# Two chunks of an attention and MLP kernel change to a seven-product scheme, with second layers in thirds

## The chip, the cores and the metric

The kernel runs on one core of one Trainium2 chip. The metric is the device time of one execution in microseconds, from runs on the chip; lower is better.

## What is computed

All arrays are float32. Four batches of eight heads (576 rows, head size 64) go through causal attention with a decay, and the 2304 x 512 result through two MLPs (512 to 1536 to 512), the second with an RMS norm ahead and a SiLU gate:

```python
scores = q @ k.T / 8 + (cum[:, None] - cum[None, :])    # cum = cumsum(log(clip(f)))
attn = softmax(where(causal, scores, -1e9)) @ v         # then rows (B*S, H*D) = (2304, 512)
x = ((x @ w_a) * (x @ w_b)) @ w_out                     # MLP 1
xn = x / sqrt(mean(x * x) + 1e-6) * rms_g
g = xn @ w_gate                                         # MLP 2
out = ((g * sigmoid(g)) * (xn @ w_val)) @ w_out2
```

The weights come as 64-bit floats. The kernel turns each granule of 128 x 512 into a high and a low 32-bit part on the chip ("decode"). A product of two such splits is made from three matmuls: high by high, high by low, low by high.

## The kernel before, in words

The rows are cut into five chunks of 576 (as 256 + 320), 512, 448, 320 and 448 (`CHUNKS`, line 23). A phase is one MLP (0 or 1) over one chunk; `PHASES` (line 33) gives their order, and this text writes them as (MLP, chunk). Activations lie transposed: features on partitions, rows as columns. A phase walks 36 granules of weights (`steps`, line 429; `plan_mlp`, line 557): 24 of the first layer, a and b in turn for 12 feature blocks f, and 12 of the second layer, three for each of four blocks of output. For every granule and sub-width the inner `block` (lines 586 to 593) issues 12 matmuls into one PSUM bank, four parts of K by three.

`gate` and `product` (lines 610 and 628) read the banks of a and b, multiply them on DVE, and `split` (line 643) writes a high part (ACT) and a low part (DVE or POOL) into the tiles `g`. All twelve f stay in SBUF until the second layer sums over them in PSUM. `out_1` keeps MLP 1's result in `x1` and adds up squares; `normed` (line 708) makes the norm of a chunk at the start of the next phase, with matmuls against ones, a Newton iteration over full tiles of 128 rows, and a new split. `out_2` sends MLP 2's result out.

`weights` (line 495) decodes a granule at its first use (load, two DVE operations, two on ACT, one on POOL) and saves it in DRAM (`wd`); later phases load it from there, 512 KB each, into a ring of five tiles. Fourteen granules of MLP 2 are decoded early, in phase (0, 1) (`EARLY`, line 39).

Attention (`plan_attention`, line 1026; `unit`, `packed`, `values`) is spread over the phases by `ATT` (line 42): the first 256 rows of batch 0 before the MLPs start, the rest of batch 0 and batch 1 in (0, 0), batches 2 and 3 over the next six phases. Each finished block is split into the tiles `x` of the chunk that it belongs to.

The order on every engine is made when the kernel is built: each operation has a cost, an engine (or a choice of two), a due time and its dependencies, and `Plan.order` (line 226) picks the operation that can start first, by due time among equals. Tiles of one tag are given out in turn. The planner treats POOL and those DVE operations that are marked `port` as excluding each other (lines 242 to 301). DMAs are all issued by SP, in that order, too.

Of the kernel before, what the change touches and what calls it, by code (L numbers as in the profile page):

```python
# [22 lines left out]
CHUNKS = [(0, (256, 320)), (576, (512,)), (1088, (448,)), (1536, (320,)), (1856, (448,))]  # L23
WIDTH = [sum(x) for _, x in CHUNKS]
N0, NMAX = CHUNKS[0][1][0], max(max(x) for _, x in CHUNKS)
PIECES = sorted({0, N0, *WIDTH})
# [6 lines left out]
PHASES = [(0, 0), (0, 1), (1, 0), (0, 2), (1, 1), (0, 3), (1, 2), (0, 4), (1, 3), (1, 4)]  # L33

LAG = 18

SLOT, HAD = [0, 1, 2, 0, 1], {3: 0, 4: 1}

EARLY = {0: 1, 1: 14}
# [3 lines left out]
    (0, ((256, 384), (384, 512), (512, 576)), ((0, 0, LAG, 1.0),), 8),  # L43
    (1, ALL, ((0, LAG, 99, 1.0),), 2),
    (2, ALL[:3], ((1, 0, 99, 0.6), (2, 0, 99, 0.5)), 0),
    (2, ALL[3:], ((3, 0, 99, 0.7), (4, 0, 99, 0.4)), 0),
    (3, ALL[:1], ((4, 18, 99, 1.0),), 0),
    (3, ALL[1:], ((5, 0, 99, 0.6), (6, 0, 99, 0.5)), 0),
# [9 lines left out]
AHEAD = [18000, 20000, 14000, 20000, 14000, 20000]  # L58
# [5 lines left out]
NORM_AT, NORM_STEPS = 6, (6, 10)  # L64
W_BUFS, W32_BUFS, A_BUFS, BP_BUFS = 5, 2, 4, 4
S_BANKS, T_BANKS, PV_BANKS, M_BANKS, BM_BANKS = 3, 1, 1, 3, 2
# [49 lines left out]
def size(c, s):  # L116
    return CHUNKS[c][1][s]


def halves_of(c, a, e):  # L120
    return [s for s in range(len(CHUNKS[c][1])) if a < half(c, s).stop and e > half(c, s).start]

# [193 lines left out]
class Kernel:  # L316
# [6 lines left out]
    def build(self):  # L323
        with ExitStack() as ctx:
            pool = lambda name, **kw: ctx.enter_context(self.tc.tile_pool(name=name, bufs=1, **kw))
            self.const, self.rot = pool("const"), pool("rot")
            self.dram, self.psum = pool("dram", space=DRAM), pool("psum", space=PSUM)
            self.plan = Plan()
# [18 lines left out]
    def m_bank(self):  # L347
        return self.bank("m", M_BANKS, pool=lambda: self.mpsum)


    def constants(self):
        nc, c = self.nc, self.const
        self.spun = self.bp.tile([128, 128], F32, name="spun")
        nc.vector.memset(self.spun, 1.0)
        self.gain = c.tile([128, KT], F32, name="gain")
        self.x1 = c.tile([128, KT, S], F32, name="x1")
# [4 lines left out]
        self.mask = self.causal(c, "mask", 128, 512)  # L361
# [46 lines left out]
    def make_x(self, pool, s):  # L408
        for t in range(2):
            for k in range(KT):  # L410
                n = max(w for w, x in zip(WIDTH, SLOT) if x == s)
                self.X[s, t, k] = pool.tile([128, n], F32R, name=f"x{s}{t}{k}")

    def make_g(self, pool, fs):
        for t in range(2):
            for f in fs:
                self.G[t, f] = pool.tile([128, S], F32R, name=f"g{t}{f}")

    def swap(self):

        for x in self.boot[::-1]:
            x.__exit__(None, None, None)
        self.mpsum = self.ctx.enter_context(self.tc.tile_pool(name="mpsum", bufs=1, space=PSUM))
        pool = self.ctx.enter_context(self.tc.tile_pool(name="late", bufs=1))
        self.make_x(pool, 2)
        self.make_g(pool, range(4, FT))


    def steps(self, p):

        both = tuple(range(len(CHUNKS[PHASES[p][1]][1])))
        if p:
            return [(j, both) for j in range(NG)]
        ab = 2 * FT
        return (
            [(j, both[:1]) for j in range(LAG)] + [(j, both) for j in range(LAG, ab)]
            + [(j, both[1:]) for j in range(LAG)] + [(j, both) for j in range(ab, NG)]
        )

    def weave(self):  # L440
        np_ = len(PHASES)
        blocks = [sum(len(subs) for _, subs in self.steps(p)) for p in range(np_)]
        extra = [[0.0] * n for n in blocks]
        for c, rows, parts, sf in ATT:
            for p, a, e, share in parts:
                span = range(a, min(e, blocks[p]))
# [4 lines left out]
        for p in range(np_):  # L451
            self.T.append([t])
            c = PHASES[p][1]
            for x, s in zip(extra[p], (s for _, subs in self.steps(p) for s in subs)):
                t += 12 * mm(size(c, s)) + x
                self.T[-1].append(t)
        self.x_parts, self.ab_blocks, self.decoded = {}, {}, set()
        self.plan_boot()
        self.op(
            DVE, dve2(128),  # L460
            lambda: self.nc.vector.tensor_scalar(
                out=self.ones, in0=self.ident, scalar1=0.0, scalar2=1.0, op0=ALU.mult, op1=ALU.add
            ),
            writes=["ones"], prio=0, start=40000,
        )
# [28 lines left out]

# [784 lines left out]
```

## Time and profile before

| what | us |
|---|---|
| median of 3 runs | 1123.12 |
| lowest and highest run | 1122.2, 1126.85 |
| span of the profiled execution, first to last instruction | 1120.8 |
| PE busy in it | 1109.3 |

The profile is one execution of the program. Its whole time is not listed apart from its span; the median of the runs is 2.3 us above that span, which is what lies around it. PE is TensorE's matmul stream, PEld its weight loads, DVE the vector engine, ACT the scalar engine, POOL GpSimd and SP the engine that issues the DMAs. Matmul records overlap, since each lasts from its issue to its modelled end while the next already runs. The pace of the stream is thus the distance of starts, not the duration.

### The profile page before, as it was taken

Reading aid. Unit: us, or ns where it says so; the run is one execution under the profiler, and the core shown is the slowest. Engines: PE = TensorE matmul, PEld = TensorE weight load, DVE = VectorE, ACT = ScalarE, POOL = GpSimd, SP = SyncE. Lnnn points to the kernel's source line nnn. Section 1 sums busy time; section 2 is a strip of 40 time slices with the busy share of each in tenths; the row PEclk is TensorE's granted clock in tenths of the full one; section 3 lists DMA queues with packets and bytes.
Section 4 is the critical chain, followed back from the end, with each engine's and each line's share of the span. In section 5 each row is a group of like instructions: output and inputs, shape, how many; then the busy total and the mean of one; then the engine's idle time right before and its main releaser. Section 6 shows DMA issues by size and latency. Waiting matters only on the chain.

```text
span 1120.8 us, 19350 instructions
## 1 busy us (share of the span) xinstructions
PE 1109.3 (99%) x7012; PEld 999.3 (89%) x7012; DVE 556.8 (50%) x1481; ACT 466.4 (42%) x1076; POOL 198.7 (18%) x245
## 2 busy tenths in 40 slices
PE   9999999999999999999999999999999999999998
PEld 7677999988889999989988778999889999999997
DVE  7877657747753877234247442544751121360330
ACT  8767557736543565333234332443441121231220
POOL 3323325412231244211011121210200000000000
PEclk9999999999999999999999999999999999999999
DMA  7879886777997488976664568787556767789774
GB/s 224 285 247 303 308 262 213 261 268 278 334 310 273 144 286 278 312 214 196 205 192 164 178 210 258 244 253 224 173 186 197 233 220 215 247 295 311 219 218 153
DMA packets 91220, 268.73 MB, mean 240 GB/s; under 512 B 14444, under 2 KB 27964, under 8 KB 91124
## 3 DMA queue, kind: packets, MB, share of 16 engines
q1 hardware_dynamic: 91124, 267.48, 73.8%
q8 instruction: 56, 0.92, 0.3%
q14 instruction: 40, 0.33, 0.1%
HBM read 224.31 MB, written 43.13 MB: 239 GB/s over the span
## 4 chain that ended last, share of the span: by engine, by line
PE 92%; DVE 4%; DMA 2%; ACT 1%; issue 0%; SPq 0%; POOL 0%; ACTq 0%; POOLq 0%
PE m L591 26%; PE m L593 26%; PE m L592 26%; PE pv L1202 4%; PE t L819 3%; PE s L1119 3%; PE s L1141 2%; PE warm L832 1%; DMA kb<-aux 1%; DMA raw<-wb 1%; DMA raw<-wa 0%; DMA qr<-qT 0%; DVE P L777 0%; DVE x L761 0%; DVE x L655 0%
## 5 line engine op out<-in xcount | busy, mean ns | idle before, releaser
L591 PE MATMUL m<-x,w 128*128 128x320 f32 (+3 forms) x1152 | 399.0, 346 | 1.2 <-DVE a L633 1.0
L593 PE MATMUL m<-x,w 128*128 128x320 f32 (+3 forms) x1152 | 388.3, 337 | 0.0
L592 PE MATMUL m<-x,w 128*128 128x320 f32 (+3 forms) x1152 | 388.0, 337 | 0.0
L591 PEld LDWEIGHTS m<-x,w 128*128 128x128 f32 x1152 | 217.1, 188 | 20.3 <-issue 4.7
L593 PEld LDWEIGHTS m<-x,w 128*128 128x128 f32 x1152 | 216.9, 188 | 13.8
L592 PEld LDWEIGHTS m<-x,w 128*128 128x128 f32 x1152 | 217.3, 189 | 13.1 <-issue 0.5
L591 PE MATMUL m<-g,w 128*128 128x320 f32 (+3 forms) x576 | 197.5, 343 | 0.0
L593 PE MATMUL m<-g,w 128*128 128x320 f32 (+3 forms) x576 | 194.1, 337 | 0.0
L592 PE MATMUL m<-g,w 128*128 128x320 f32 (+3 forms) x576 | 194.0, 337 | 0.0
L633 DVE TENSOR_TENSOR a<-m,a 128x320 f32<-128x320 f32 (+3 forms) x144 | 79.7, 555 | 175.2 <-PE m L593 167.5
L649 ACT ACTIVATE g<-a 128x320 fp32r<-128x320 f32 (+3 forms) x144 | 75.0, 521 | 157.3 <-DVE a L633 157.1
L505 POOL TENSOR_TENSOR w<-w,w 128x512 fp32r<-128x512 f32 x72 | 98.8, 1375 | 219.3 <-ACT w L502 170.0
L615 ACT ACTIVATE a<-m 128x320 f32<-128x320 f32 (+3 forms) x144 | 70.3, 489 | 112.3 <-PE m L593 111.0
L591 PEld LDWEIGHTS m<-g,w 128*128 128x128 f32 x576 | 108.6, 188 | 8.0 <-issue 1.2
L593 PEld LDWEIGHTS m<-g,w 128*128 128x128 f32 x576 | 108.5, 188 | 6.8
L592 PEld LDWEIGHTS m<-g,w 128*128 128x128 f32 x576 | 108.6, 189 | 6.4
L652 DVE TENSOR_TENSOR g<-a,g 128x320 fp32r<-128x320 f32 (+3 forms) x139 | 84.4, 608 | 50.5 <-ACT g L649 49.7
L784 ACT ACTIVATE P<-P,mn 128x512 f32<-128x512 f32 (+4 forms) x128 | 76.1, 595 | 37.2 <-DVE mn L777 36.8
L777 DVE CUSTOM_DVE_ANT_0 P<-s,mask 128x512 f32<-128x512 f32 (+4 forms) x128 | 61.7, 497 | 48.3 <-PE s L1141 24.1
L1183 ACT ACTIVATE pt<-t 128x384 f32<-128x384 f32 (+4 forms) x105 | 51.5, 490 | 58.4 <-PE t L819 57.7
L1063 POOL TENSOR_SCALAR qa<-qr 64x384 fp32r<-64x384 f32 (+4 forms) x38 | 19.2, 506 | 317.6 <-PE s L1119 198.4
L622 DVE SCALAR_TENSOR_TENSOR a<-a,m 128x256 f32<-128x256 f32 (+3 forms) x72 | 39.7, 551 | 62.3 <-ACT a L615 60.6
(105 smaller groups left out, 1115.8 us busy)
## 6 DMA issues: line engine op xcount, KB each, us to landing
w<-wd SPq DMA_DIRECT2D x321, 512.0 KB
wd<-w SPq DMA_DIRECT2D x72, 512.0 KB
raw<-wo SPq DMA_DIRECT2D x24, 512.0 KB
raw<-wa SPq DMA_DIRECT2D x12, 512.0 KB
raw<-wb SPq DMA_DIRECT2D x12, 512.0 KB
raw<-wg SPq DMA_DIRECT2D x12, 512.0 KB
raw<-wv SPq DMA_DIRECT2D x12, 512.0 KB
vr<-vA SPq DMA_DIRECT2D x32, 128.0 KB
```

The costliest lines, as they stand in the source:

```text
L505: nc.gpsimd.tensor_tensor(out=w.tile[:, 1, :], in0=i32.tile.bitcast(F32), in1=w.tile[:, 0, :].bitcast(F32), op=ALU.subtract)
L591: nc.tensor.matmul(o, w.tile[:, 0, wc], xh, start=kt == 0, stop=False)
L592: nc.tensor.matmul(o, w.tile[:, 0, wc], xl, start=False, stop=False)
L593: nc.tensor.matmul(o, w.tile[:, 1, wc], xh, start=False, stop=kt == last)
L615: ACT, act(n, 1), lambda x: nc.scalar.activation(x[:, :n], acc.tile[:, :n], func, scale=scale),
L633: nc.vector.tensor_tensor(out=a.tile[:, :n], in0=acc.tile[:, :n], in1=a.tile[:, :n], op=ALU.mult)
L649: nc.scalar.activation(out(0), x(), AF.Copy, **({} if scale is None else {"scale": scale}))
L652: self.engine(by).tensor_tensor(out=out(1), in0=x(), in1=out(0).bitcast(F32), op=ALU.subtract)
L777: nc.vector.tensor_tensor_reduce(out=p.tile[:n, i * w : i * w + w], in0=s[i].tile[:n, :w], in1=masks[i][:n], scale=-0.125, scalar=mn.tile[ ...
L784: nc.scalar.activation(o, o, AF.Exp, bias=mn.tile[:n, len(s) - 1 : len(s)], scale=-1.0, accum_out=x[:n])
L1183: nc.scalar.activation(x.tile[:r, :to], ps.tile[:r, :to], AF.Copy)
L1202: nc.tensor.matmul(x[64 * g : 64 * g + 64, o : o + n], tiles[g][2][0].tile[:k, i, :], y.tile[:k, to : to + n], start=i == 0, stop=i == blo ...
```

## The change

There are three chunks, of 576 (256 + 320), 704 (two halves of 352) and 1024 rows (two halves of 512), and six phases: (0, 0), (0, 1), (1, 0), (1, 1), (0, 2), (1, 2).

In the chunks of 704 and 1024 the first layer is done by a Strassen scheme (in Winograd's form). For one f the two weight granules, each cut in two halves of K, are the four blocks of a 2 x 2 matrix; the activations, cut in two halves of K and two of the rows, are the four blocks of the other. Seven products of six matmuls (`P1` to `P7`, two parts of K by three) take the place of eight such groups. The sums of activation blocks are made once for a phase (`expand`: four additions and seven splits into "cells" of twice the half's width). The sums of weight blocks are made per f (`sums`) in (0, 1) and (1, 1), from the two decoded granules, and saved in DRAM (`ws`); (0, 2) and (1, 2) load them. The sums of products are formed in part by accumulating in PSUM, in part by DVE on tiles copied out by ACT.

The second layer runs in thirds of K: after four f the four output blocks are made over these four and added to `xc` by DVE, so that `G` holds only four f. The last third of (1, 1) is done behind (0, 2) ("held"). The norm adds up columns with fp32 matmuls of one column, iterates on 3 or 4 numbers per partition, and spreads the result with fp32 matmuls over diagonals. The ring of weight tiles goes from five to seven, the banks of scores from three to two, those of MLP products from three to four (`m1` two, `m2` and `m3` one each). No granule of MLP 2 is decoded early. Attention ends in (1, 1); its tiles then make room for the wide chunk (`swap_2`, `swap_3`). Attention's result for chunks 1 and 2 is copied once, not split.

```diff
-CHUNKS = [(0, (256, 320)), (576, (512,)), (1088, (448,)), (1536, (320,)), (1856, (448,))]
+CHUNKS = [(0, (256, 320)), (576, (352, 352)), (1280, (512, 512))]
...
-PHASES = [(0, 0), (0, 1), (1, 0), (0, 2), (1, 1), (0, 3), (1, 2), (0, 4), (1, 3), (1, 4)]
+PHASES = [(0, 0), (0, 1), (1, 0), (1, 1), (0, 2), (1, 2)]
+SUMS_IN, AHEAD = (1, 3), {0: (), 2: ()}
+THIRDS, QF = 3, FT // 3
...
+    (0, ((256, 384), (384, 512), (512, 576)), ((0, 0.0, 0.33, 1.0),), 8, 18000),
+    (1, ALL, ((0, 0.33, 0.85, 1.0),), 2, 5000),
+    (2, ALL[:1], ((0, 0.85, 0.93, 1.0),), 0, 5000),
+    (2, ALL[1:], ((1, 0.1, 1.0, 0.6), (2, 0.0, 0.2, 0.4)), 0, 5000),
+    (3, ALL, ((2, 0.1, 1.0, 0.7), (3, 0.1, 0.95, 0.3)), 0, 20000),
...
-W_BUFS, W32_BUFS, A_BUFS, BP_BUFS = 5, 2, 4, 4
-S_BANKS, T_BANKS, PV_BANKS, M_BANKS, BM_BANKS = 3, 1, 1, 3, 2
+EARLY = {1: (0, 0, 0.3, 1.0)}
+HELD = 3
+SWAP_AT = 4
+W_BUFS, W32_BUFS, A_BUFS, BP_BUFS = 7, 4, 7, 4
+S_BANKS, T_BANKS, PV_BANKS, BM_BANKS = 2, 1, 1, 3
+M_BANKS = {"m1": 2, "m2": 1, "m3": 1}
...
+    def blocks(self, p):
+
+        m, c = PHASES[p]
+        n = range(len(CHUNKS[c][1]))
+        if c == 0:
+            if p:
+                return [x for q in range(THIRDS) for x in self.plain_blocks(q, n)]
+            some = [(q, ss) for ss in ([0], [0, 1], [1]) for q in ((2,) if len(ss) > 1 else (0, 1))]
+            return [x for q, ss in some for x in self.plain_blocks(q, ss)]
+        out = [("P1", 0), ("P7", 0), ("P2", 0)]
+        for f in range(FT):
+            out += [("P6", f), ("P4", f)]
+            nxt = [[(x, f + 1)] if f + 1 < FT else [] for x in ("P1", "P7", "P2")]
+            out += [*nxt[0], ("P5", f), *nxt[1], *nxt[2], ("P3", f)]
+            if f % QF == QF - 1 and not (p == HELD and f == FT - 1):
+                out += [("y", i, f // QF, s) for i in range(KT) for s in n]
...
+        if p == HELD + 1:
+            out += [("held", i, THIRDS - 1, s) for i in range(KT) for s in range(len(CHUNKS[PHASES[HELD][1]][1]))]
+        return out
...
+    def sums(self, m, f, ws, t):
...
+            def whole(by, i32=i32, w=w):
+                y = [w.tile[:, :, h, :].bitcast(F32) for h in range(2)]
+                self.engine(by).tensor_tensor(out=i32.tile.bitcast(F32), in0=y[0], in1=y[1], op=ALU.add)
...
+        for d, out, a, b, how, r, wr in (
+            (0, a22, a21, a22, ALU.add, k21, k22), (1, a21, a11, a21, ALU.subtract, k11, k21),
+            (2, a11, a22, a11, ALU.subtract, k22, k11), (3, a12, a12, a11, ALU.subtract, k11, k12),
+        ):
...
+            op(EITHER, (dve(256), pool2(256)), go, reads=[r], writes=[wr], prio=t - 8600 + 100 * d, port=True)
...
+            op(ACT, act(512), high, reads=keys, writes=[(y, 0)], prio=t - 7000 + 500 * x)
+            op(EITHER, (dve(512), pool2(512)), low, reads=[*keys, (y, 0)], writes=[(y, 1)], prio=t - 6500 + 500 * x, port=True)
...
+        use = {"P1": ("one", 0, B11), "P7": (0, 0, T3), "P2": ("one", 1, B21), "P6": (1, 0, T2), "P4": ("two", 1, T4),
+               "P5": (0, 1, T1), "P3": (1, 1, B22)}
+        on = {"P1": "m1", "P7": "m2", "P2": "m3", "P6": "m1", "P4": "m2", "P5": "m1", "P3": "m1"}
...
+            def block(*_, w_=w_, bank_=bank_, idx=idx, b=b, start=start, stop=stop):
+                for k in range(2):
+                    self.triple(
+                        bank_.tile[:, :h], w_, idx, k, self.cell(b, 0, c, m)[:, k, :], self.cell(b, 1, c, m)[:, k, :],
+                        start and k == 0, k == 1, skip_group_check=True,
+                    )
...
+        def sums():
+            for i, a in enumerate(at):
+                nc.tensor.matmul(r.tile[:, i : i + 1], total()[:, a : a + 128], self.spun[:, 0:1], start=True, stop=True)
...
+        def spread():
+            for i in range(k):
+                x = diag(i) if i in whole else rest.tile[:, :128]
+                nc.tensor.matmul(bc.tile[:, at[i] : at[i] + 128], self.spun, x, start=True, stop=True)
```

## Rows read from the trace of the kernel before

**Rows 1.** Page: busy us of each engine, share of the span, instructions.

```profile
PE 1109.3 (99%) x7012; PEld 999.3 (89%) x7012; DVE 556.8 (50%) x1481; ACT 466.4 (42%) x1076; POOL 198.7 (18%) x245
```

**Rows 2.** Waits of PE, first and last of nine: us in total, times, longest.

```profile
PE s L1141 <- DMA kb<-aux: 1.5, 2, 0.9
...
PE t L905 <- DVE bP L900: 0.3, 1, 0.3
```

**Rows 3.** Stages; busy us of PE, PEld, DVE, ACT, POOL; PE clock, DMA share, GB/s.

```profile
29.55:107.70 78.15, 74.76 (x575) 57.70 (x575) 59.74 (x184) 56.90 (x134) 22.63 (x19) 0.98 0.85 276
107.70:236.37 128.67, 128.13 (x1058) 121.57 (x1056) 85.69 (x268) 80.60 (x203) 47.53 (x49) 1.00 0.78 262
236.37:347.16 110.79, 110.25 (x539) 89.83 (x537) 66.01 (x169) 54.42 (x120) 26.85 (x30) 1.00 0.87 300
347.16:473.90 126.74, 125.90 (x963) 124.09 (x962) 80.07 (x184) 63.91 (x141) 40.40 (x39) 1.00 0.76 259
473.90:577.71 103.81, 103.81 (x609) 93.49 (x608) 37.27 (x91) 30.59 (x65) 13.48 (x24) 1.00 0.65 199
577.71:689.84 112.13, 111.22 (x544) 89.83 (x543) 53.28 (x135) 35.58 (x82) 18.32 (x41) 1.00 0.64 199
689.84:774.09 84.25, 84.25 (x662) 81.26 (x660) 40.64 (x129) 36.20 (x91) 12.07 (x17) 1.00 0.80 243
774.09:877.82 103.73, 103.73 (x597) 93.94 (x596) 47.39 (x121) 34.36 (x78) 6.98 (x9) 1.00 0.62 195
877.82:965.37 87.55, 87.55 (x433) 81.15 (x432) 16.27 (x26) 16.98 (x31) 0.00 (x0) 1.00 0.70 220
...
1029.55:1120.80 91.25, 87.71 (x434) 80.94 (x432) 22.45 (x36) 16.11 (x29) 0.00 (x0) 0.99 0.66 206
```

**Rows 4.** Timeline of PE at three widths: start, us, instruction.

```profile
304.28 0.39 PE L592 MATMUL m<-x,w 128*128 128x512 f32 x1
...
306.58 0.39 PE L593 MATMUL m<-x,w 128*128 128x512 f32 x1
...
400.20 0.31 PE L592 MATMUL m<-x,w 128*128 128x320 f32 x1
...
401.23 0.31 PE L593 MATMUL m<-x,w 128*128 128x320 f32 x1
401.37 0.28 PE L591 MATMUL m<-x,w 128*128 128x256 f32 x1
...
402.69 0.28 PE L593 MATMUL m<-x,w 128*128 128x256 f32 x1
```

**Rows 5.** Chain that ended last: start, us, what; the fp32 warm matmuls.

```profile
1.05 5.84 PE warm L832 x26
```

**Rows 6.** Lines kept apart by shape: busy us, mean ns; idle before.

```profile
L502 ACT ACTIVATE w<-w 128x512 fp32r<-128x512 f32 x72 | 45.3, 629 | 40.8 <-DVE w L538 27.6 <-PE m L593 9.3 <-issue 2.0
L633 DVE TENSOR_TENSOR a<-m,a 128x448 f32<-128x448 f32 x48 | 29.9, 623 | 114.7 <-PE m L593 114.6
L633 DVE TENSOR_TENSOR a<-m,a 128x320 f32<-128x320 f32 x48 | 23.3, 486 | 28.5 <-PE m L593 23.3 <-issue 2.9 <-PE t L819 2.1
L633 DVE TENSOR_TENSOR a<-m,a 128x512 f32<-128x512 f32 x24 | 16.6, 690 | 26.6 <-PE m L593 24.1 <-ACT w L530 2.3
...
L592 PEld LDWEIGHTS m<-x,w 128*128 128x128 f32 x1152 | 217.3, 189 | 13.1 <-issue 0.5
```

**Rows 7.** Chain that ended last, two waits for granules: start, us, what.

```profile
25.06 5.81 DMA raw<-wb
...
89.10 5.20 DMA raw<-wa
```

**Rows 8.** Timeline of DVE and POOL: start, us, instruction.

```profile
60.05 1.28 POOL L505 TENSOR_TENSOR w<-w,w 128x512 fp32r<-128x512 f32 x1 [2.50 <-ACT w L502]
60.75 0.87 DVE L652 TENSOR_TENSOR g<-a,g 128x256 fp32r<-128x256 f32 x1 [1.16 <-ACT g L649]
...
391.20 0.43 DVE L652 TENSOR_TENSOR g<-a,g 128x256 fp32r<-128x256 f32 x1
```

More of the change, by code (lines that the diff above doesn't have):

```diff
@@ L424, in swap @@
         pool = self.ctx.enter_context(self.tc.tile_pool(name="late", bufs=1))
[L425 to L438, printed above, removed]
+        self.G.append(pool.tile([128, 8 * NARROW], F32R, name="G"))
@@ new lines, in triple, with y_block, block @@
+    def triple(self, o, w, i, k, xh, xl, start, stop, **more):
+        mm_ = partial(self.nc.tensor.matmul, **more)
+        wh, wl = (w.tile[:, i, h, k * 128 : k * 128 + 128] for h in range(2))
+        mm_(o, wh, xh, start=start, stop=False)
+        mm_(o, wh, xl, start=False, stop=False)
+        mm_(o, wl, xh, start=False, stop=stop)
+    def y_block(self, p, c, i, q, s, w, acc, t, e, first, last, m, after=()):
+        cols, n = half(c, s), size(c, s)
+        for a, b in ((0, QF - 1), (QF - 1, QF)):
+            def block(*_, a=a, b=b):
+                for k in range(a, b):
+                    x = [self.g(t, k, c, cols) for t in range(2)]
+                    self.triple(acc.tile[:, :n], w, k // 2, k % 2, *x, k == 0, k == QF - 1)
+            reads = [x for t_ in range(2) for k in range(a, b) for x in self.g_keys(t_, k, c, cols)]
+            made = self.op(
+                PE, 3 * (b - a) * mm(n), block, reads=["late", (w, 0), (w, 1), *reads], writes=[acc],
+                prio=t + 3000 + 0.75 * (e - t) * (a > 0), after=after,
+            )
+        self.out_part(p, m, c, i, s, first, last, acc, e)
+        return made
@@ new lines, in normed, with step @@
+        h, v, q = (lambda i=i: small.tile[:, i, :k] for i in range(3))
+        bits = lambda x: x().bitcast(I32)
+        def step(eng, cost, fn, reads, writes, dt, port=True):
+            op(eng, cost, lambda *a: fn(), reads=reads, writes=writes, prio=t0 + dt, port=port)
+        def scalars(out, x, a, b, op0, **op1):
+            nc.vector.tensor_scalar(out=out, in0=x, scalar1=a, scalar2=b, op0=op0, **op1)
+        def sums():
+            for i, a in enumerate(at):
+                nc.tensor.matmul(r.tile[:, i : i + 1], total()[:, a : a + 128], self.spun[:, 0:1], start=True, stop=True)
@@ new lines, in normed, with scaled @@
+        reads = [(each, i) for i in whole]
+        if len(whole) < k:
+            rest = y
+            step(DVE, dve2(128), over, [small], [rest], 3000 + 100 * k)
+            reads.append(rest)
+        step(PE, 216 * k, spread, ["late", *reads], [bc], 4000)
+        if late:
+            src, key = bc, [bc]
+        else:
+            step(ACT, act(n, 1), lambda: nc.scalar.activation(y.tile[:, :n], bc.tile[:, :n], AF.Copy), [bc], [y], 5000)
+            src, key = y, [y]
+        for i in range(KT):
+            def scaled(i=i):
+                x = self.xc[c][:, i, cols]
+                nc.vector.scalar_tensor_tensor(
+                    out=x, in0=x, scalar=self.gain[:, i : i + 1], in1=src.tile[:, :n], op0=ALU.mult, op1=ALU.mult
+                )
+            step(DVE, dve(n), scaled, [*key, "gain"], pieces(c, s, "x1", c, i), 6000 + 1000 * i, not late)
```

828 lines of the change are left out of this document (548 added, 280 removed).

## The prediction

> **What bounds the kernel now.** Read the busy times first [rows 1]: TensorE is busy 99% of the span, its weight loads 89%, the next engine (DVE) 50%. A busy matmul row can hide a slow stream, so two more views are needed. The waits of PE [rows 2] are nine kinds; summed they are 7.6 us, none above 1.5 us. The stages [rows 3] show where PE is not full: 3.4 us in the first stretch, where POOL, ACT, DVE and DMA decode weights while attention runs (DMA 0.85), and 3.5 us after the last matmul; a phase without attention, old (0, 4), has no idle time. The spacing of matmuls in the timeline [rows 4] shows that the stream itself is at its rate: 11 steps in 1.32 us at 256 columns (0.120 us each), 7 in 1.03 at 320 (0.147), 10 in 2.30 at 512 (0.230), and 432 matmuls of 448 in the 87.55 us of old (0, 4) (0.2027). These lie on a line; 352 columns, which the trace lacks, come to 0.161 by interpolation between 320 and 448. The bound is the count of columns that PE streams, so a change that cuts columns pays one for one until another engine is late.
>
> **Matmuls removed.** Before, each MLP pass over one chunk is 432 matmuls (36 granules x 12) per sub-width. For both MLPs: 2 x 432 x (0.120 + 0.147 + 0.230 + 0.2027 + 0.147 + 0.2027) = 906.7 us. After, chunk 0 keeps 432 each at 256 and 320; the chunks of 704 and 1024 take 12 f x 7 products x 6 = 504 for the first layers (instead of 576) and 288 for the second, 792 matmuls of 352 and of 512. Sum: 2 x [432 x 0.267 + 792 x (0.161 + 0.230)] = 850.0 us. Term: **-56.6 us**. Bounds: if 352 cost as 320 does, the term is -79; if as 448, it is +9; four widths on one line speak for the middle.
>
> **Norm on PE.** Removed: 12 matmuls against ones, about 2.1 us at the spacings above. Added: a column sum and a spread by diagonals, 38 fp32 matmuls (per half 2, 3, 3, 3, 4, 4 blocks, twice). The nearest row is the fp32 128x128 warm matmul, 26 in 5.84 us, 0.225 each [rows 5]: 8.5 us, all on PE. Term: **+6.4** (between 2, if the one-column sums cost as little as a transpose, and 8). The 0.8 us that PE idled in old (1, 0) [rows 3], a phase with a norm, goes, since the new chain works on 3 or 4 numbers per partition: -0.8.
>
> **New vector work: price and cover.** Records of neighbours on DVE overlap by about 0.08 us, so occupancy is taken 0.08 below the duration. From [rows 6]: DVE two-input 512 wide 0.61, 352 wide 0.44, 256 wide 0.34 (the last from the uncontended row in [rows 8]); POOL 512 wide 1.28 [rows 8]. One f in the first-layer scheme costs DVE four reads of PSUM (1.76), one product and two low parts (1.3); in MLP 2 two gates more (0.9). Phases (0, 1) and (1, 1) also make the weight sums: per f four 256-wide adds (1.36), two low parts (1.2), two whole adds (2.6 on POOL or 1.2 on DVE), two ACT copies of 0.63. DVE per f: 5.6 in MLP 1, 6.5 in MLP 2, without the whole adds. PE per f: 42 x 0.161 = 6.76, plus attention, an estimate from [rows 3]: the six old phases from (0, 1) to (1, 2) hold batches 2 and 3 and last 11.4 + 11.4 + 16.2 + 12.7 + 20.8 + 16.1 = 88.6 us longer than their matmuls, some 5 us of norm and waits in it; so a batch is about 41, and batch 2 without its first and smallest row block about 37. With 0.6 of 37 in (0, 1) and 0.3 of 41 in (1, 1), spread evenly, PE per f is 7.9 and 7.4 outside the second layers. DVE fits, barely; the second layers, PE 15.5 us per third for about 6 of DVE, give the room back. The wide phases have no attention: 9.7 us of PE per f against 4.2 to 5.4 of DVE. These all count nothing, by that cover.
>
> **New waits.** The trace does not show the scheme, so these are bounded by rows.
> 1. First stretch: chunk 0's first half now needs 24 decoded granules, not 18, before its second half starts. The old stretch took 78.2 us for 18 (4.3 us each) with DMA at 0.85 [rows 3], and PE filled it with attention of batch 1, of which some 41 us are there. +3 (0 to 10).
> 2. Decode of MLP 2: before, 14 of 36 granules ran in (0, 1); now all 36 run in (1, 0), beside attention of two batches. PE there is 115.3 + 0.4 x 37 + 0.7 x 41 + 2.6 = 161 us. Old (0, 0) held 36 decodes beside some 90 us of attention with DVE at 145 of 207 us [rows 3]; half that attention, with the gates and the cells of (1, 1) on top, makes some 125 of 161 (estimate). +2 (0 to 8).
> 3. Weight tiles: f needs four of the seven in the ring (two halves loaded, two sums made), so the load for f+2 waits until product P5 of f has read its tile. From there to P7 of f+2: landing 5.2 [rows 7], a whole add 1.28, two adds 0.68, ACT 0.63, DVE 0.61, handoffs some 0.8: 9.2 us. Seven products (6.8) lie between, six more (5.8) until P5 of f+2, so two f take 16 us where PE alone needs 13.5: 1.2 per f, 29 for 24 f. The attention of these two phases, 22 + 12 us, can stand in the gaps, save after each y group, where y tiles hold the ring and one gap of some 5 us opens, four in all. Below: 0, if the order written by the planner turns P5 and P7 round; above: each step behind another instruction, 13.2 us instead of 9.2, 3.2 per f, 77 less 33 of attention. I take +9, near the lower end, since the cover is nearly the whole.
> 4. End of (1, 1): its last y group is moved behind (0, 2), so nothing covers the 11 vector operations 1024 wide (1.15 each on the line of [rows 6], 12.6 us) that make the cells for chunk 2; three cells lie on tiles that the last products still read. +5 (0 to 15).
> 5. Wide phases: after a y group a load waits for P5 of the next f: about 5.2 of landing against three products of 1.39. Four times 1: +4 (0 to 12). Between (0, 2) and (1, 2) the 15.5 us of held y blocks cover the norm and the first cells: +1.
> PE's queue is in order, so behind each such wait stand all later matmuls, and nothing else on the chip makes up the time. DMA falls by about 36 MB (465 weight transfers become some 396 of 512 KB), no term.
>
> **Sum,** against the profiled span of 1120.8: 1120.8 - 56.6 + 6.4 - 0.8 + 24 = 1093.8. The median of the runs, 1123.1, is 2.3 above that span, so the forecast is **1096**, own range 1084 to 1108.
>
> **A rule weighed.** DVE's record L652 of 256 columns took 0.87 us while a POOL subtraction ran from 60.05 to 61.33, and 0.43 in a stretch without POOL [rows 8]: it waited. The Trainium skill (SBUF — State Buffer, the section on engine ports) says that a DVE operation with two SBUF inputs and a GpSimd operation exclude each other for their whole length. The trace agrees. The planner's order knows such a lock (lines 242 to 301), so my sum takes only its leftovers.
>
> **Rivals.**
> (B) The planner hides nearly all: of the 24 us of new waits 4 stay. For it: the old order has 11.5 us of idle time in 1120.8. Against it: old phases had no chain of load, sum, split and product. 1076.
> (C) The shared port paces (1, 1). Operations that exclude each other, per f: POOL 2.56, DVE adds 1.36, low parts of sums 1.2, product, low parts and gates 2.2, attention's own about 0.65: 8.0 against 7.4 (6.76 and 12 us of attention spread over the phase): +7 in 12 f; at its end the 12.6 us of cells cannot share with POOL: +8 more. 1111. For it: the row just named. Against it: the whole adds may go to DVE.
> (D) Slower: the tile chain of point 3 at its upper price. Two f take 13.2 + 6.8 = 20 us, 24 f lose 77 and attention fills 33: 44 in place of 9, 1131. It decides against the change from a chain of about 13 us on. For it: landing of 5.2 to 5.8 [rows 7] under load, and these phases move 2.1 MB per f. Against it: every step would have to queue. A rival that the change does not do what it says, that 352 columns run no faster than the weight load: a load's record is 0.189 long [rows 6], yet 320 columns step by 0.147 [rows 4], so loads do overlap; no chance of its own.
>
> **How the numbers follow.** Forecast 0.48, B 0.22, C 0.18, D 0.12. About 0.5% is what a measurement of this kernel can tell from no change, so faster means below 1117.5 and slower above 1128.7. Faster: the forecast, B and 0.15 of C: 0.85. Same: 0.03 of C and 0.02 of D: 0.05. Slower: 0.10 of D. The range 1073 to 1122 leaves out most of D, the lower edge of B and the upper of C, about 0.17.
>
> **What the changed profile would show.** Matmul records fall from 5184 to 4896 in the MLPs, spaced 0.161 at 352. A wide phase lasts 183 us plus about 2 of waits, (0, 1) about 152, (1, 0) about 163. Right on waits: PE waiting for DVE or ACT results made from weight sums in (0, 1) and (1, 1), mostly right after y groups, and at the start of (0, 2). Point 3 is wrong if PE shows no such wait; C is right if POOL and DVE records in (1, 1) stretch against each other while PE waits; D is right if each f there takes 10 us. A step of 352 far from 0.161 would make the whole sum wrong.

## The result and the profile after

The changed kernel takes **1130.66 us** (median of 14 runs, 1124.77 to 1135.53), the kernel before beside it 1123.13 (14 runs, 1119.62 to 1132.01): a ratio of 1.0053, 95% interval 1.0031 to 1.0075. That is slower by about half a per cent, small but beyond the interval; 1096 was forecast, within 1084 to 1108. Its profiled execution took 1133.41 us with a span of 1131.2; the sum in the prediction stands against spans.

The page of the changed kernel, its busy times and the granted clock in 40 slices:

```profile
span 1131.2 us, 19154 instructions
PE 1080.2 (95%) x6794; PEld 953.5 (84%) x6794; DVE 761.1 (67%) x1860; ACT 555.2 (49%) x1227; POOL 216.5 (19%) x245
PEclk9998999999999999999999999899999999999999
PE 60%; DVE 18%; DMA 12%; ACT 4%; issue 3%; SPq 1%; POOL 0%; DVEq 0%; ACTq 0%; POOLq 0%
```

Against [rows 1], PE lost 29 us of busy time and VectorE gained 204. But PE's idle time went from 11.5 us to 51.0, so the span did not fall. The last line is the chain of work that ended last: PE holds only 60% of it, VectorE 18% and DMAs 12%.

The stages of the changed kernel (length; busy us and instructions of PE, PEld, DVE, ACT, POOL; granted clock, DMA share, GB/s): chunk 0 in MLP 1, then (0, 1), (1, 0), (1, 1), (0, 2) with the held blocks, (1, 2) to the end, and the last 27.9 us of (1, 1) by themselves.

```profile
33.10:255.10 222.00, 210.41 (x1660) 182.06 (x1660) 152.14 (x479) 145.53 (x361) 75.84 (x95) 0.98 0.77 252
255.13:424.20 169.07, 160.22 (x1059) 150.47 (x1058) 138.72 (x355) 89.18 (x201) 37.00 (x44) 0.99 0.64 219
424.20:594.91 170.71, 164.36 (x1335) 156.12 (x1333) 142.93 (x388) 111.58 (x258) 76.03 (x71) 0.99 0.68 228
594.91:731.62 136.71, 127.81 (x829) 121.65 (x828) 111.25 (x249) 71.87 (x156) 16.17 (x19) 0.98 0.65 223
731.62:938.00 206.38, 204.91 (x940) 171.13 (x940) 100.42 (x173) 54.23 (x88) 0.00 (x0) 0.99 0.50 159
938.00:1131.20 193.20, 183.95 (x793) 149.16 (x791) 92.90 (x133) 58.43 (x95) 0.00 (x0) 0.99 0.46 145
703.70:731.60 27.90, 21.75 (x116) 19.77 (x115) 24.30 (x48) 12.79 (x25) 0.00 (x0) 0.92 0.59 213
```

(0, 1) was to last about 152 us and lasts 169; (1, 0) 163, and lasts 171. In (0, 1) and (1, 1) VectorE is busy 82% and 81% of the time: a chain that was to hide in the gaps finds that engine occupied. The two wide phases, without sums, are nearer the forecast, some 4 us above it each (183 us and about 2 of waits; (0, 2) also holds 17 us of held blocks).

The matmul streams themselves do as priced. PE's timeline, the first and the last record of an unbroken run at either width:

```profile
308.16 0.33 PE L765 MATMUL m<-E,w 128*128 128x352 f32 x1
...
314.35 0.32 PE L765 MATMUL m<-G,w 128*128 128x352 f32 x1
...
738.41 0.40 PE L765 MATMUL m<-E,w 128*128 128x512 f32 x1
...
777.75 0.39 PE L767 MATMUL m<-E,w 128*128 128x512 f32 x1
```

39 steps in 6.19 us are 0.159 each, and 173 in 39.34 are 0.227; the sum had 0.161 and 0.230. So the step was not what failed. But not all of the loss is idle time: PE's busy time fell by 29.1 us where the two PE terms of the sum, -56.6 and +6.4, are 50.2. Some 21 us of the miss thus stand inside PE's busy rows, as matmuls at the lower clock (the last section has an example) and, it is argued, as stalls so short that the overlap of records covers them; how they divide was not isolated. PE's recorded waits in (1, 1), the first three kinds (us in total, times, longest):

```profile
PE m L765 <- ACT w L678: 4.5, 2, 3.3
PE m L765 <- DVE a L1005: 1.5, 2, 0.7
PE t L1240 <- ACT pt L1604: 0.8, 2, 0.6
```

L678 is the high part of a weight sum. The longest of these waits, followed back, in the chain of the changed kernel from 716 us on (start, us, what):

```profile
716.35 6.32 DMA w<-wd
722.67 0.02 issue
722.69 0.69 DVE w L651
723.39 1.14 DVE E L885
724.52 0.34 DVE w L670
724.86 1.13 DVE xc L875
725.99 0.34 DVE w L670
726.33 0.43 DVE a L1046
...
727.72 0.66 PE m L765
```

From the load on this is the chain of point 3 of the new waits: load, whole add, small adds, the copy of the high part, product. It takes 11.4 us from issue to product, not 9.2. What releases PE is ACT's copy L678, which needs the first two small adds alone; what VectorE does from 726.33 on runs beside it. ACT's timeline:

```profile
726.09 1.06 ACT L882 ACTIVATE E<-xc 128x1024 fp32r<-128x1024 f32 x1 [3.04 <-DVE xc L875]
727.05 0.61 ACT L678 ACTIVATE w<-w 128x512 fp32r<-128x512 f32 x1
```

The second small add ends at 726.33, but ACT has just begun L882 and takes the copy up 0.72 us later. So 5.0 us lie behind the landing, and 3.0 of them are steps that are not of the sum: L885 (1.14) and L875 (1.13) on VectorE and L882 on ACT. All three make chunk 2's cells, and of the two phases with sums only the end of (1, 1) has that work, so the chain need not be as long elsewhere. The load took 6.32 us where [rows 7] had 5.81 and 5.20; two other loads on the chain in this phase took 4.07 and 6.15.

The chain's beginning is not the one that point 3 described. There the load waits until a product has read its tile. SP's timeline (its issues of DMAs), and what SP waited for in the whole of (1, 1):

```profile
700.20 0.32 SPq L933 DMA_DIRECT2D w<-wd  x1
711.68 1.52 SPq L688 DMA_DIRECT2D ws<-w  x2
713.25 0.45 SPq L933 DMA_DIRECT2D w<-wd  x1
715.93 0.32 SPq L688 DMA_DIRECT2D ws<-w  x1
716.35 0.37 SPq L933 DMA_DIRECT2D w<-wd  x1
SPq L688 <- DVE w L681: 53.6, 17, 11.1
SPq L933 <- PE m L767: 32.3, 17, 5.8
SPq L688 <- DVE w L670: 17.5, 4, 8.6
```

SP issues the DMAs in the planned order. From 700.5 to 711.7 us it stood at a store of a finished sum (L688, `ws`) until VectorE had made its low part, and no load was issued. The loads at 713.25 and 716.35 each follow such a store, and the trace has no wait of theirs for PE. In all of (1, 1) SP waited 71 us at these stores and 32 us for products to free tiles (L933). So two things hold a load back: the ring of tiles, and the store of an earlier sum that stands before it in SP's queue. The prediction had the first alone.

The Trainium skill (SBUF — State Buffer, the section on the DMA setup-cost knee) fits a transfer as about 2 us plus its bytes over 436 GB/s, with an approximation at middle sizes admitted. By that page of the Trainium skill 512 KB would land in 3.2 us, an estimate. The trace disagrees for a queue in use: 6.32 us here.

### The profile page after: what moved, and what is told of

Its sections match the earlier page's. It is cut to its first block, busy times and chain, and to the rows that moved or that the text cites. A ratio compares the mean times of both kernels' runs of the same rounds, so it can differ in the third digit from the quotient of the medians.

```text
span 1131.2 us, 19154 instructions
## 1 busy us (share of the span) xinstructions
PE 1080.2 (95%) x6794; PEld 953.5 (84%) x6794; DVE 761.1 (67%) x1860; ACT 555.2 (49%) x1227; POOL 216.5 (19%) x245
## 4 chain that ended last, share of the span: by engine, by line
PE 60%; DVE 18%; DMA 12%; ACT 4%; issue 3%; SPq 1%; POOL 0%; DVEq 0%; ACTq 0%; POOLq 0%
PE m L765 18%; PE m L767 18%; PE m L766 17%; DMA w<-wd 3%; DMA raw<-wo 3%; PE pv L1623 3%; PE s L1540 2%; PE t L1240 2%; DVE w L617 2%; DVE P L1198 2%; DVE w L670 1%; DVE E L885 1%; DVE w L651 1%; DMA raw<-wb 1%; DVE a L1005 1%
## 5 line engine op out<-in xcount | busy, mean ns | idle before, releaser
L765 PE MATMUL m<-E,w 128*128 128x512 f32 (+3 forms) x1056 | 365.4, 346 | 16.3 <-ACT w L678 4.5
L767 PE MATMUL m<-E,w 128*128 128x512 f32 (+3 forms) x1056 | 356.1, 337 | 0.3 <-DVE w L681 0.2
L766 PE MATMUL m<-E,w 128*128 128x512 f32 (+3 forms) x1056 | 354.8, 336 | 0.5 <-DVE E L885 0.5
L765 PEld LDWEIGHTS m<-E,w 128*128 128x128 f32 x1056 | 200.9, 190 | 39.4 <-ACT w L678 6.0
L766 PEld LDWEIGHTS m<-E,w 128*128 128x128 f32 x1056 | 201.0, 190 | 16.0 <-DVE E L885 1.4
L767 PEld LDWEIGHTS m<-E,w 128*128 128x128 f32 x1056 | 200.3, 190 | 16.1 <-DVE w L681 2.1
L1005 DVE TENSOR_TENSOR a<-m,a 128x352 f32<-128x352 f32 (+1 forms) x192 | 115.3, 604 | 130.8 <-PE m L767 127.2
L765 PE MATMUL m<-G,w 128*128 128x352 f32 (+3 forms) x576 | 199.3, 346 | 4.1 <-ACT xc L805 1.4
L767 PE MATMUL m<-G,w 128*128 128x352 f32 (+3 forms) x576 | 194.0, 337 | 0.0
L766 PE MATMUL m<-G,w 128*128 128x352 f32 (+3 forms) x576 | 193.9, 337 | 0.0
L1097 ACT ACTIVATE G<-a 128x352 fp32r<-128x352 f32 (+3 forms) x144 | 75.0, 521 | 127.7 <-DVE a L1005 87.1
L996 ACT ACTIVATE a<-m 128x352 f32<-128x352 f32 (+1 forms) x144 | 75.0, 528 | 114.4 <-PE m L767 113.3
L765 PEld LDWEIGHTS m<-G,w 128*128 128x128 f32 x576 | 108.5, 188 | 16.3 <-ACT xc L805 2.2
L766 PEld LDWEIGHTS m<-G,w 128*128 128x128 f32 x576 | 108.6, 189 | 9.3 <-DVE G L1100 1.2
L767 PEld LDWEIGHTS m<-G,w 128*128 128x128 f32 x576 | 108.4, 188 | 8.5 <-POOL w L625 0.2
L1100 DVE TENSOR_TENSOR G<-a,G 128x512 fp32r<-128x512 f32 (+3 forms) x134 | 79.6, 596 | 51.0 <-ACT G L1097 49.1
L1240 PE MATMUL t<-ident,P 128*128 128x128 f32 (+1 forms) x376 | 64.5, 278 | 13.3 <-DVE pt L1606 4.6
L1604 ACT ACTIVATE pt<-t 128x512 f32<-128x512 f32 (+4 forms) x106 | 50.7, 478 | 25.8 <-PE t L1240 25.1
```

What stands on the lines that cost most here:

```text
L765: mm_(o, wh, xh, start=start, stop=False)
L766: mm_(o, wh, xl, start=False, stop=False)
L767: mm_(o, wl, xh, start=False, stop=stop)
L996: nc.scalar.activation(z[:, :h], bank_.tile[:, :h], AF.Copy)
L1005: nc.vector.tensor_tensor(out=z, in0=bank_.tile[:, :h], in1=z, op=ALU.mult if mult else ALU.add)
L1097: nc.scalar.activation(out(0), x(), AF.Copy)
```

## The experiments

In the expectations theory 2 is the chain of weight tiles; other theories put the cost on the load of the vector work alone, on the first stretch, or on other places, as each text says. Lengths of phases from PE's timelines of the profiled executions (first product to first product, the last to the last matmul; "start" is the time before the first; (0, 2) holds 17 us of held blocks where there are any):

| kernel | ratio to before | start | (0,0) | (0,1) | (1,0) | (1,1) | (0,2) | (1,2) |
|---|---|---|---|---|---|---|---|---|
| after | 1.0053 | 33.1 | 222.0 | 169.0 | 170.8 | 136.7 | 206.3 | 189.5 |
| e1 sums left out | 0.9782 | 32.0 | 216.0 | 161.8 | 164.7 | 123.8 | 205.2 | 190.5 |
| e2 sums made for nobody | 0.9859 | 32.8 | 218.3 | 162.1 | 165.8 | 126.5 | 205.1 | 189.4 |
| e3 one third first | 0.9942 | 35.0 | 209.9 | 169.8 | 170.4 | 136.2 | 205.3 | 190.5 |
| e4 no held blocks | 1.0104 | 33.3 | 217.8 | 173.5 | 169.8 | 152.5 | 184.9 | 197.9 |
| e5 ring of six | 1.0361 | 33.0 | 215.8 | 181.4 | 164.5 | 155.0 | 209.7 | 197.2 |
| e6 P5 earlier | 0.9904 | 33.4 | 218.5 | 173.0 | 161.3 | 130.4 | 205.7 | 186.9 |
| e7 wholes kept | 0.9947 | 32.1 | 232.1 | 164.4 | 163.4 | 128.3 | 203.2 | 189.9 |
| e8 three edits | 0.9885 | 33.5 | 212.8 | 170.9 | 168.9 | 129.4 | 207.3 | 187.0 |
| e9 e6 without sums | 0.9802 | 33.1 | 220.8 | 161.4 | 169.0 | 124.1 | 202.8 | 187.7 |
| e10 e6 and e7 | 0.9990 | 31.7 | 239.8 | 163.1 | 166.7 | 128.2 | 202.8 | 188.0 |

Each row is one execution, and one execution says little about a few us in one phase. The changed kernel and e4 have the same instructions in the same order on every engine up to 657 us, and yet (0, 0) is 4.2 us shorter in e4 and (0, 1) 4.5 longer. The changed kernel and e1 agree so up to 184 us, where the changed kernel is already 7.0 us later; their PE records are the same even up to these two, the first of the changed kernel, the second of e1:

```profile
205.59 0.31 PE L767 MATMUL m<-E,w 128*128 128x320 f32 x1
198.61 0.31 PE L767 MATMUL m<-E,w 128*128 128x320 f32 x1
```

So what a change costs is read from the medians and ratios, and the table only for where it lies. The profiled execution of the changed kernel is 2.8 us above its median, that of e1 3.3 below.

**e1: the weight sums left out.** The two tiles that were summed are filled by plain loads of 512 KB, and nothing is stored for the wide phases.

```diff
-            make = (m, f) not in self.summed and p in SUMS_IN
+            make = False
...
-                key, src, cut = ("ws", m, f, kind), self.ws[m][f][kind], 0
+                key, src, cut = ("wd", m, 2 * f + kind), self.wd[m][2 * f + kind], 0
```

> Leaves the weight sums out: the five products that need them read decoded granules in their place, loaded from DRAM as in the wide phases; no sums are made or saved. The changed kernel ran 1131 us, some 60 above its columns at full rate. Theory 1 (vector load: DVE is full in (0, 1) and (1, 1) because of the sums' 100 us of records): (0, 1) falls from 169 to about 153 us, (1, 1) from 137 to about 126, the whole to about 1103. Theory 2 (tile chain: load, sum, split, product through seven tiles): the same, about 1103. Theory 3 (the loss is elsewhere: first phase, (1, 0), clock): above 1118.

Measured: 1102.91 us, ratio 0.9782 (0.9734 to 0.983). The whole of (1, 1) and its last 27.9 us:

```profile
574.50:698.30 123.80, 123.41 (x829) 120.32 (x827) 73.42 (x163) 54.59 (x120) 8.20 (x8) 1.00 0.63 204
670.40:698.30 27.90, 27.90 (x172) 27.43 (x171) 18.50 (x31) 9.66 (x19) 2.81 (x2) 1.00 0.73 241
```

PE has 0.4 us of idle time in (1, 1) where it had 8.9, and none at its end, though the cells of chunk 2 are made there just the same. The sums cost 28 to 30 us (by medians and by ratios). In the spans 33.4 us lie between the two kernels. 7.2 + 12.9 of them lie in the phases that make sums. The 6.0 of (0, 0) are not the sums' doing: they are there while both kernels still run the same instructions. Of the 6.1 of (1, 0) little can be said, since e9, also without sums, has 169.0 there.

**e2: the sums' vector work without anyone waiting.** e1 with the same adds, copies and low parts on scratch tiles.

```diff
+    def load_only(self, f, t):
...
+            if name == "P7" and p in SUMS_IN:
+                self.load_only(f, t)
```

> As e1 without the sums, but the same vector and ACT operations are done per f in (0, 1) and (1, 1) on scratch tiles that no product waits for. Theory 1 (vector load): nearly all of e1's gain is gone again, 1120 to 1130. Theory 2 (tile chain): e1's gain stays, within 8 us of e1, about 1105 to 1111. Theory 3: like e1, above 1118 both.

Measured: 1109.31 us, 0.9859 (0.9799 to 0.9919). Its (1, 1):

```profile
579.00:705.50 126.50, 124.48 (x830) 119.99 (x829) 106.37 (x234) 67.51 (x149) 21.59 (x24) 1.00 0.61 198
```

VectorE is nearly as busy as after the change (106.4 against 111.3 us), and the phase is 10.2 us shorter. So of the sums' cost 6 to 9 us are the load, though the intervals of e1 and e2 overlap, and 21 to 22 (by either measure) hang on products and stores that need the results. The waits on record hold only part of that: PE's for L678 are 4.5 us, all in (1, 1). In (0, 1) the trace has no wait for L678. There attention's 244 matmuls take 31.0 us from each start to the next, and in e2 242 of them take 22.6. So in that phase attention did not fill the gaps but was itself held up.

e2 also leaves out the 48 stores of sums (25 MB; 43.1 MB written against 68.3), as e1 does, and with them SP's 71 us of waits in (1, 1). So e1 and e2 do not tell the ring of tiles from these stores. e7 has the stores and brings (1, 1) to 128.3, with 36 us of such waits left there: it speaks against their traffic as the cause, not against their place before the loads. No run moved the stores alone.

**e3: one third before the second half, not two.** The first stretch needs 12 granules for its first half instead of 24; attention is spread to match.

```diff
-    (0, ((256, 384), (384, 512), (512, 576)), ((0, 0.0, 0.33, 1.0),), 8, 18000),
-    (1, ALL, ((0, 0.33, 0.85, 1.0),), 2, 5000),
+    (0, ((256, 384), (384, 512), (512, 576)), ((0, 0.0, 0.167, 1.0),), 8, 18000),
+    (1, ALL, ((0, 0.167, 0.85, 1.0),), 2, 5000),
...
-            some = [(q, ss) for ss in ([0], [0, 1], [1]) for q in ((2,) if len(ss) > 1 else (0, 1))]
+            some = [(q, ss) for ss in ([0], [0, 1], [1]) for q in ((1, 2) if len(ss) > 1 else (0,))]
```

> Only the first third of K goes ahead for the first half of chunk 0 (8 granules and 4 y blocks) instead of two thirds; the rest runs for both halves; attention of batches 0 and 1 is spread to match. If the first phase lost its 11 us because 24 granules must be decoded before batch 0's second half may start: (0, 0) falls from 222 to about 213 us, the whole to about 1122. If that loss has another cause (two score banks, the y adds): no change, 1128 to 1134. If attention before block 12 is now the tight one: slower, up to 1140.

Measured: 1122.05 us, 0.9942 (0.991 to 0.9975). That is 9 to 12 us less (by medians and by ratios), as expected. (0, 0) falls from 222.0 to 209.9, the start grows by 1.9; beside the other kernels with the old order, at 215.8 to 220.8, the fall in (0, 0) is smaller. The first stretch costs some 10 us more than the order needs: point 1 was near the upper end of its range, not its +3.

**e4: no held blocks.** The last y group of (1, 1) stays in (1, 1).

```diff
-HELD = 3
+HELD = -9
```

> The last third of the second layer of (1, 1) is put back to its place at the end of (1, 1) instead of behind (0, 2). If the bare start of (0, 2) costs what the trace suggests (6 us of idle time and a granted clock of 0.92 and 0.97 there): that comes back, about -8. Against it the norm between (0, 2) and (1, 2) loses its 17 us of cover: about +10. Expected 1128 to 1140; below 1125 would show that the held blocks were a mistake.

Measured: 1136.44 us, 1.0104 (1.007 to 1.0137). As expected, the held blocks are worth having, by 5.8 us, though the intervals of the two ratios just touch: without them (1, 2) is 8.4 us longer, while (1, 1) and (0, 2) together are 5.6 shorter.

**e5: a ring of six weight tiles.**

```diff
-W_BUFS, W32_BUFS, A_BUFS, BP_BUFS = 7, 4, 7, 4
+W_BUFS, W32_BUFS, A_BUFS, BP_BUFS = 6, 4, 7, 4
```

> The ring of weight tiles is six instead of seven; nothing else changes, no vector operation is added. Theory 2 (tile chain; each f holds four tiles and the next f's loads wait for them): (0, 1) and (1, 1) grow by 15 to 25 us each, the wide phases by less, the whole to 1165 to 1185. Theory 1 (vector load): no change, 1128 to 1136.

Measured: 1165.09 us, 1.0361 (1.0311 to 1.041). One tile less costs 34 us, the lower edge of what theory 2 had. The phases with sums grow most, by 12.4 and 18.3, the wide ones by 3.4 and 7.7; but (0, 1) holds 44 more of attention's matmuls here and (1, 0), 6.3 shorter, 42 fewer, so (0, 1) alone grew by less than the 15 to 25 expected. PE's waits in its (1, 1), the first of them:

```profile
PE m L765 <- ACT w L678: 10.5, 5, 3.9
PE m L765 <- DVE a L1005: 2.5, 3, 1.1
```

The very wait of the changed kernel, 4.5 us in 2 there, is 10.5 us in 5 here: 6 of the 34. So the number of tiles matters, as theory 2 has it, and theory 1 does not explain it.

**e6: the block that frees the tile is moved up, the block that needs the sum down.** P3 moves up too, and P7 and P2 change places; the work is the same.

```diff
-            out += [*nxt[0], ("P5", f), *nxt[1], *nxt[2], ("P3", f)]
+            out += [("P5", f), *nxt[0], ("P3", f), *nxt[2], *nxt[1]]
```

> Only the order of the products is changed: P5 and P3 of f, which read the two sums of f, come before P7 and P2 of f+1, so the tiles of f's sums are free two to three products earlier. The same operations on every engine. Theory 2 (tile chain): (0, 1) and (1, 1) together 6 to 10 us shorter, the whole about 1122 to 1125. Theory 1 (vector load): no change, 1128 to 1136.

Measured: 1112.81 us, 0.9904 (0.9871 to 0.9938), less than both kernels. Between P5 of f and P7 of f + 2 stand eleven products instead of seven, 4 x 6 x 0.159 = 3.8 us more. The gain, some 17 us, is larger than expected, and it is not where it was expected. Its (1, 1), and what PE waits for there:

```profile
586.10:716.50 130.40, 124.63 (x824) 119.73 (x823) 108.22 (x238) 70.01 (x153) 20.99 (x24) 0.99 0.64 228
PE m L765 <- ACT w L678: 3.6, 2, 3.2
```

The phase is 6.3 us shorter, (1, 0) before it 9.5, and (0, 1) 4.0 longer: (0, 1) and (1, 1) together gain 2.3, not 6 to 10. (0, 1) holds 34 more of attention's matmuls than in the changed kernel and (1, 0) 33 fewer, so these two are read together, 5.5 shorter. Of the 18.4 us between the spans 3.2 are there at 272 us already, up to which the two kernels run the same instructions in the same order. One wait of 3.2 us on L678 stays, and SP's waits at the stores in (1, 1) stay at 70 us.

**e7: the joined weights kept, so no whole adds.** The decode stores each joined granule; the sums load it.

```diff
+                op(SP, 480, keep, reads=both, writes=[("wf", m, j)], prio=t - 5000, nbytes=262144)
...
-                (POOL, DVE), (pool2(512), dve(512)), lambda *a, whole=whole: whole(a[0]), reads=[(w, 0), (w, 1)],
-                writes=[(i32, k) for k in range(2)], prio=t - 10000, port=True,
+                SP, 480, lambda *_, i32=i32, j=j: nc.sync.dma_start(i32.tile.bitcast(F32).rearrange("p a b -> p (a b)"), self.wf[m][j]),
+                reads=[("wf", m, j)], writes=[(i32, k) for k in range(2)], prio=t - 18000, nbytes=262144,
```

> The joined weights are saved in DRAM at the decode (256 KB for each of 48 granules) and loaded for the sums, so the 48 whole additions go (31 us of DVE records) and the sums no longer wait for the granules' own tiles; 48 stores and 48 loads of 256 KB are added. Theory 1 (vector load): a third of the sums' records gone, -8 to -12 in (0, 1) and (1, 1). Theory 2 (tile chain): 1 to 2 us off each chain, but the two tiles of the sums still wait for the ring: -3 to -8; (1, 0) may grow by the stores. The whole 1118 to 1128.

Measured: 1118.71 us, 0.9947 (0.992 to 0.9975). The first add goes, and with it the wait of the sums' load for a tile of the ring: it lands in a tile outside the ring. (0, 1), (1, 0) and (1, 1) are 4.6, 7.4 and 8.4 us shorter, and (0, 0), which has half of the 48 new stores, is 10.1 longer. The 13.0 of (0, 1) and (1, 1) are more than the 3 to 8 of theory 2 and just above the 8 to 12 of theory 1. e7 takes away vector work, a step of the chain and a wait for the ring at once, and halves 24 loads; it does not decide between them.

**e8: e3, e6 and a third bank for the y blocks together.**

```diff
-                tags = ("m2", "m3") if q < THIRDS - 1 else ("m2", "m3", "m1", "m1")
+                tags = ("m2", "m3", "m1") if q < THIRDS - 1 else ("m2", "m3", "m1", "m1")
```

> The edit of e3 (first third), that of e6 (P5 earlier), and a third bank in turn for the y blocks of the first two thirds (m2, m3, m1 instead of m2, m3), which gives each y block one more block of time to be read out. e3 gave -9 and e6 is expected to give -7; the third bank takes part of the 0.9 us that each y group of the wide phases loses: -3. The whole 1109 to 1116, below both kernels. If the wide phases lose for another reason, 1115 to 1120.

Measured: 1113.08 us, 0.9885 (0.9846 to 0.9925). The number lies within what was expected, but the gains do not add: (0, 0) is 5.7 shorter than in e6, but (1, 0) gives 7.6 back. Against e6 this is no change.

**e9: the order of e6 where there are no sums.** Both edits of e1, and:

```diff
-            out += [*nxt[0], ("P5", f), *nxt[1], *nxt[2], ("P3", f)]
+            out += [("P5", f), *nxt[0], ("P3", f), *nxt[2], *nxt[1]]
```

> The weight sums left out as in e1, and the block order of e6 with them. The output is not the reference's: the seven products read joined weights in place of the sums. It asks what the order of e6 works through. Theory 2 (the order gives the chain of sums more time between the block that frees a tile and the block that needs the next sum): without sums there is no chain, and the order should gain little, 1098 to 1104 us against 1102.9 of e1, with (0,1) and (1,1) at 160 to 163 and 122 to 125 us. Rival (the order pays outside the sums, by spreading the seven products' combinations on VectorE between the blocks): it gains here what it gained in e6, 15 to 20 us, 1083 to 1090 us.

Measured: 1102.43 us, 0.9802 (0.9775 to 0.983), against 0.9782 of e1. (0, 1) is 161.4 and (1, 1) 124.1. An order that gains 17 us with sums gains nothing without them: it works through the sums, as theory 2 has it, and not by spreading the combinations. Whether through the ring or through SP's queue it does not tell.

**e10: e6 and e7 together,** the edits of both, the first of them:

```diff
-            out += [*nxt[0], ("P5", f), *nxt[1], *nxt[2], ("P3", f)]
+            out += [("P5", f), *nxt[0], ("P3", f), *nxt[2], *nxt[1]]
...
-        for w in ws:
+        for j in ws:
```

> The block order of e6 and the joined weights kept from the decode as in e7. Alone, e6 measured 1112.8 and e7 1118.7 us against 1130.7. If the two took time out of the same chain, the second edit finds little left: 1108 to 1115 us, as its stores lengthen the first phase by 10 us. If they took it from different places the gains add: about 1100 us (1097 to 1104).

Measured: 1124.8 us, 0.999 (0.9971 to 1.0009): a miss of both expectations. (0, 1) and (1, 1), 163.1 and 128.2, are within 1.3 us of e7 and far below e6 in (0, 1), which fits two edits that took their time from one chain. But (0, 0) is 239.8 us, 7.7 above e7 and 21.3 above e6, and that eats the gain. The windows of the first stretch, this kernel's:

```profile
31.70:130.00 98.30, 86.53 (x623) 65.17 (x622) 60.79 (x192) 62.79 (x146) 32.83 (x30) 0.93 0.84 279
```

PE idles 11.8 us of 98 there, at a granted clock of 0.93. The new order is not the reason that the phase is longer than e7's: the two kernels run the same instructions in the same order on every engine up to 257 us of e7, and there e10 is already 7.3 us later. What made these executions differ is open.

## Why the prediction was wrong

**The step that failed** is point 3 of the new waits. It priced the chain at 9.2 us, saw that it could reach 13.2 "each step behind another instruction", and then took +9 of a possible 44 "since the cover is nearly the whole". The chain measured 11.4 us where it was followed, and e2 puts what hangs on the sums' results at 21 to 22 us. Three parts of the step failed:

- The steps of the chain: the landing took 6.3 us, not 5.2, and 3.0 us of foreign work stood between the steps, on engines that were priced as free. (The whole add was cheaper than priced, 0.7 on VectorE, and the low part is not on the chain.)
- The beginning: the load was to wait for P5 alone. In the trace it also stands behind the stores of sums in SP's queue, 71 us of SP's waits in (1, 1) against 32 for the tiles. The prediction had no such wait.
- The cover: attention was to stand in the gaps. In (0, 1) its matmuls took 8.4 us longer than in e2 instead. That this is because attention itself needs VectorE is argued, not shown.

e5 and e9 show that the ring and the order of products matter through the sums. How the 21 to 22 us divide between the ring and the stores is not shown.

**Rival D** had the chain and the number: 1131 against 1130.7 measured. The agreement of the number is luck: D put 44 us on the chain, half of that was measured, and other terms made up the rest. Its chance of 0.12 was too low; "every step would have to queue" was said against it, and in the chain followed most of the steps do queue. Its sign, 10 us per f, is met in (0, 1) (10.3 without the y groups), but e1 has 9.7 there without any sums, and (1, 1) has 8.8.

**Matmuls removed, -56.6:** right, and low. At 0.159 and 0.227 per step the two new widths are 2 x 792 x 0.005 = 8 us cheaper still; 0.227 is also the median step of 512 columns before, so that the saving is larger by some 5 us.

**Norm on PE, +6.4:** right. Its 38 matmuls take 7.8 us from each start to the next (their overlapping records add up to 10.0); 8.5 were priced.

**New vector work, nothing:** not nothing. e2 against e1 is 6 to 9 us of load. The whole adds were priced for POOL or VectorE; the planner put 46 of 48 on VectorE:

```profile
L651 DVE TENSOR_TENSOR w<-w 128x512 f32<-128x512 f32 x46 | 31.6, 689 | 10.0 <-DMA w<-wd 9.6
L651 POOL TENSOR_TENSOR w<-w 128x512 f32<-128x512 f32 x2 | 2.8, 1407 | 16.7 <-DVE w L670 16.2 <-DMA w<-wd 0.5
```

For the same reason rival C did not come: POOL is busy 16 us of the 137 of (1, 1).

**Point 1, +3:** about +10, its upper end. e3 takes out 9 to 12 us by this order alone, and 3.5 more are lost before it, where the first matmul of an MLP starts at 33.1 instead of 29.55.

**Point 2, +2:** (1, 0) lasts 170.8, 161 were priced for PE. Over all the runs it lasts 161.3 to 170.8, and 164.7 and 169.0 in the two kernels without sums, so this point is 0 to 10 us, and what of it comes with the sums is not shown.

**Point 4, +5:** 6.2 us idle in the last 27.9 of (1, 1), as priced, but not for the cells by themselves. e1 makes them too and has none. In the chain above they cost by standing between the steps of a sum.

**Point 5, +5:** PE idles 1.5 us in (0, 2) and 5.5 in (1, 2) before its end: 7, about right.

**The clock** had no term. Its mean fell from 0.998 to 0.989. It is 0.92 in the 27.9 us above, of which PE was busy 21.75, while e1 has 1.00 in the last 27.9 us of its (1, 1). One per cent of 1131 us bounds what this added at some 10 us; no run changed it alone.

Set against 1120.8 - 56.6 + 6.4 = 1070.6, the span shows 60.6 us of excess, where 24 less 0.8 were forecast. The sums are 28 to 30 of it, the first stretch about 10 (the two may overlap, since the gains of e3 and e6 did not add in e8), and the rest the start, point 5, and (0, 1), which lasts 161.8 us even in e1 where 152 were named, with 4.3 us of idle time and a clock of 0.98. What is shown is that the sums' results cost 21 to 22 us beyond their vector work (e2), that the ring (e5) and, through the sums, the order of products (e6 with e9) bear on it, and the first stretch (e3). What is open is the part of the stores in SP's queue.

## What to carry to other kernels

When a scheme trades matmuls for sums made on the way, price the chain from the read that frees a buffer to the product that needs the refilled one, with every step behind other work of its engine, and compare it with the work that really stands between the two in PE's order. Follow the chain back through the queue that issues the loads, too: there a store that waits for a result holds up every load behind it. Do not count work that fills PE as cover for a chain on VectorE before looking at what else that work waits for; here attention was held up along with the products. What helped most was order, not less work: four products more between the freeing block and the needing one took out some 17 us, and the kernel came out 1% below the one before. And before a difference between two phases is explained, check that the two kernels differ there at all.

## What the runs showed of the hardware

A mean granted clock below 1 was not expected in a kernel whose PE is busy 95% of the time. Between its two levels, 1.2 and 2.4 GHz, it averages 0.98 of the full one in (1, 1) and 0.92 in its last 27.9 us, where PE had waited 6.2 us; where e1 takes the waits away the last 27.9 us of the phase are at 1.00. Before and after the wait of 3.3 us that ended at 727.72:

```profile
720.00:724.30 4.30, 4.30 (x28) 4.11 (x26) 4.06 (x8) 1.85 (x4) 0.00 (x0) 1.00 0.94 380
728.00:733.90 5.90, 5.90 (x18) 5.11 (x19) 4.41 (x7) 2.84 (x6) 0.00 (x0) 0.50 0.45 179
```

PE is busy throughout both, at 2.4 GHz in the first and at 1.2 GHz in the second. So here a wait cost somewhat more than its length, and the surplus stands in busy time.

Of two 512 KB loads on the chain in (1, 1), where the DMAs were busy 0.65 of the time, one landed in 6.32 us and one in 4.07. The mean share of the phase does not tell them apart. The share in each load's own time, 0.92 and 0.75, goes with the landing, as far as two loads can show:

```profile
716.35:722.67 6.32, 6.19 (x39) 6.22 (x40) 6.10 (x13) 3.67 (x9) 0.00 (x0) 1.00 0.92 294
595.82:599.89 4.07, 2.51 (x15) 1.74 (x14) 2.91 (x7) 2.99 (x8) 3.80 (x6) 1.00 0.75 239
```
